# First Q and K weights issued by ScalarE, VectorE's constants first, and a new written order of all engines

## The chip, the cores and the metric

The kernel runs on one core of a Trainium2 chip. The metric is the device time of one execution in microseconds; the kernel before takes 200.04 (median of 3 runs, 199.62 to 200.08). One further execution was taken with the hardware profiler.

The core has TensorE (PE, matrix products; PEld is its weight load), VectorE (DVE), ScalarE (ACT), GpSimd (POOL), and SyncE (SP), which here issues the DMAs. Each engine works through its own instructions in order.

## The reference

Two branches work on the same input x (A_x) and are mixed by a gate:

```python
qkv = (x @ wqkv)                              # x: 2048 x 512, 32 heads of 16
scores = einsum("bhqd,bhkd->bhqk", q, k) * 16 ** -0.5
scores = where((0 <= i - j) & (i - j < 256), scores, -1e9)
a = (softmax(scores) @ v) @ wo                # sliding window of 256
h = layernorm(x)
u = gelu(einsum("bsd,sf->bdf", h, w1) + b1)   # 2048 -> 1376, over tokens
b = transpose(einsum("bdf,fs->bds", u, w2) + b2)
g = sigmoid((x * gate_w).sum(-1))
out = g * a + (1 - g) * b
```

## The kernel before

**Tiling.** The 2048 tokens are 16 tiles of 128. Projections work on four blocks i of 512 tokens: `q{k}_{i}` and `k{k}_{i}` for four groups k of eight heads, and `v{t}` for each tile t. Each is a chain of four matmuls over 128 rows of the weights, accumulated in one PSUM bank (`chain`, L691). In block 0 the first matmul is split into two halves of 256 columns, so that its steps `.0` and `.1` need different halves of x. Copies bring the results out: `kc`, `vc` and `xtc` (`copy_out`, L637, on VectorE or ScalarE) and `qc` (VectorE, L792).

**Attention.** For each tile j, scores `s{j}.v0` to `.v3` and the corner `s{j}.C` go to pairs of PSUM banks; ScalarE takes the exponential of each pair (`e...`, L932); VectorE or GpSimd puts zeros outside the window (`m...`, L945, L1012, L571); the products with V (`pv{j}.n`, L1125) follow. V parts that must lie on other partitions are moved by DMA within SBUF: `vs{t}` (L756) and `vz{j}` (L766), which wait for the V tiles that they move. VectorE then normalises and transposes the result (`n1` to `n4`, `nz`, L1216 to L1251) for the product with `wo`.

**The other branch.** `bs`, `ba`, `pow`, `h` are the layernorm. `u0` to `u10` multiply h by w1 over the tokens; `ub` adds the bias; one `gelu` task (L1291) works on all of them in place. It needs another table of ScalarE than the exponentials. `y{t}` multiplies by w2, and its last four matmuls by wo, so one bank holds both branches; `f{t}` scales and `o{t}` stores. The gate is the VectorE product `gl{t}` (L860) with a copy of gate_w on all partitions (`gw`, loaded at L542), a sum in the same instruction, then a small exponential `gatee`.

**The order.** Every piece of work is a `Task` with its engine's cost. The order on each engine, the choice of VectorE, ScalarE or GpSimd where there is one, and the bank or buffer (the digits behind the colon) are written out in `PLAN` (L217). [...] The costs are no instructions. On an engine the order is exactly that of `PLAN`: a task whose input is late holds everything behind it, and this goes for SyncE's queue of loads too.

**The start.** SyncE issues x in two halves of a block (x0.0, x0.2: tokens 0 to 255 and 256 to 511), then wqk0 to wqk3, each 128 rows of the Q and K weights (256 KB), with x1.4 (512 KB) between wqk2 and wqk3; then gw, wv and the DMA transposes xt1, xt3, xt2 of the other blocks. TensorE warms up on zeros (`warm`, five matmuls of 512 columns), transposes block 0 itself (`xta0.n.g`: half n of x, half g of its columns), with three matmuls on zeros (`warmb`) between the halves, and goes into the projections of block 0.

Of the kernel before, what the change touches and what calls it, by code (L numbers as in the profile page):

```python
# [9 lines left out]
ACT = mybir.ActivationFunctionType  # L10
# [92 lines left out]

def arrange(tasks):
# [21 lines left out]
    while len(order) < len(tasks):  # L126
# [92 lines left out]
        warm:5 xta0.0.1:4 xta0.0.0:3 warmb xta0.1.1:4 xta0.1.0:5 q2_0.0:6 q3_0.0:0 k1_0.0:2 k3_0.0:3  # L219
        k0_0.0:1 q1_0.0:5 q1_0.1 k2_0.0:7 q0_0.0:4 k2_0.1 q2_0.1 k0_0.1 q0_0.1 k3_0.1 k0_0.2 q0_0.2 k1_0.1  # L220
        q0_0.3 k3_0.2 q1_0.2 k3_0.3 q1_0.3 q3_0.1 q2_0.2 k1_0.2 q1_0.4 k1_0.3 q0_0.4 k0_0.3 k3_0.4 q2_0.3
        k0_0.4 q3_0.2 q2_0.4 k2_0.2 k1_0.4 k2_0.3 k2_0.4 v1.0:1 q3_0.3 q3_0.4 s0.v0:24 v1.2 v0.0:7 q3_1.0:6
        v0.2 q3_1.2 s0.C:24 v5.0:0 k2_1.0:7 k2_1.2 v5.2 s-1.C:24 v3.0:6 v14.0:7 v14.2 s1.v3:04 biast:3 v3.2
        q1_1.0:7 q1_1.2 s1.v0:02 v2.0:6 v2.2 v12.0:4 v12.2 v4.0:5 v4.2 pv-1.0:0 s0.v1:26 k3_1.0:4 k3_1.2
        k3_2.0:5 s1.v2:06 k3_2.2 v6.0:2 q0_1.0:3 q0_1.2 v6.2 pv0.0:0 pv0.1 pv0.2 s1.v1:46 v7.0:3 v7.2
        v15.0:2 s2.v1:06 v15.2 k0_2.0:5 v13.0:4 k0_2.2 v13.2 k1_1.0:3 s1.C:06 k2_2.0:2 k2_2.2 k1_1.2
        s2.v3:06 k0_1.0:5 k0_1.2 v10.0:2 v10.2 pv1.0:0 pv1.1 pv1.2 pv1.3 s2.v0:46 pv1.4 v8.0:2 v8.2 v9.0:3
        v9.2 s2.v2:06 q2_1.0:5 k1_2.0:4 q2_1.2 s2.C:20 k1_2.2 u0.0:6 u0.2 v11.0:7 v11.2 s3.v1:40 u0.4 u0.6
        u0.8 s3.C:02 u2.0:7 u0.10 u2.2 u0.12 u2.4 s3.v2:42 pv2.0:0 u0.14 pv2.1 pv2.2 pv2.3 u2.6 u2.8
        s3.v0:24 u1.0:6 u1.2 u1.4 s3.v3:02 u1.6 u1.8 u2.10 s4.v0:42 u2.12 u1.10 u2.14 u1.12 u1.14 s4.v1:04  # L230
        pv3.0:2 pv3.1 pv3.2 pv3.3 u3.0:7 u3.2 u3.4 s5.v2:04 u3.6 u3.8 u3.10 s4.v3:20 u3.12 u3.14 u4.0:6 u4.2
        s4.v2:24 q0_2.0:7 q0_2.2 u4.4 s4.C:40 u4.6 u4.8 u4.10 s6.v0:02 u4.12 q3_2.0:7 u4.14 pv4.0:4 pv4.1
        pv4.2 pv4.3 s5.v0:02 u5.0:6 q3_2.2 u5.2 u5.4 s5.v1:42 u5.6 u5.8 q2_2.0:7 q2_2.2 s5.C:02 u5.10 u5.12
        u5.14 s6.C:04 u6.0:7 u6.2 u6.4 s6.v2:02 u6.6 u6.8 q1_2.0:6 q1_2.2 u6.10 s5.v3:04 u6.12 u6.14 u7.0:6
        s6.v1:02 u7.2 u7.4 pv5.0:4 pv5.1 pv5.2 pv5.3 s6.v3:02 u7.6 u7.8 k3_3.0:7 k3_3.2 s7.v0:04 u7.10
        pv6.0:2 pv6.1 u7.12 pv6.2 pv6.3 s7.v1:04 u8.0:7 u7.14 u8.2 s7.v3:02 u8.4 k1_3.0:6 k1_3.2 s7.C:04
        u8.6 u8.8 q0_3.0:6 s7.v2:42 q0_3.2 u8.10 u8.12 u8.14 s8.v3:20 u9.0:6 u9.2 u9.4 s8.C:04 u10.0:7 u10.2
        u10.4 s8.v1:24 u9.6 u9.8 u10.6 u9.10 s8.v0:20 u9.12 u10.8 u9.14 s8.v2:42 u10.10 pv7.0:0 pv7.1
        q1_3.0:6 u10.12 u10.14 q1_3.2 s10.v0:24 pv7.2 k2_3.0:7 k2_3.2 pv8.0:2 pv8.1 k0_3.0:6 pv8.2 pv8.3
        pv7.3 k0_3.2 q2_3.0:4 q2_3.2 q3_3.0:5 y4.0:6 y0.0:7 q3_3.2 s9.v1:02 y0.2 y0.4 y4.2 y4.4 y0.6 y4.6  # L240
        y0.8 y0.10 s9.v3:40 y0.11 y0.13 y4.8 s9.v2:02 y4.10 y4.11 y2.0:7 y2.2 s9.C:40 y2.4 y4.13 y2.6
        s9.v0:24 y2.8 y2.10 y7.0:6 y2.11 s10.C:04 y2.13 y7.2 y7.4 s10.v3:02 y7.6 y8.0:7 y8.2 s11.v3:04 y8.4
        y7.8 pv9.0:2 pv9.1 pv9.2 pv9.3 s10.v2:04 y7.10 y8.6 y8.8 y8.10 s10.v1:02 y8.11 y8.13 y7.11 s11.C:04
        y7.13 y1.0:7 y1.2 y1.4 s11.v2:02 y5.0:6 y1.6 y5.2 s11.v1:24 y1.8 y5.4 y5.6 s13.v3:20 y1.10 y5.8
        pv10.0:4 pv10.1 pv10.2 y1.11 y1.13 y5.10 pv10.3 s12.v2:02 y5.11 y9.0:7 y5.13 s12.v0:04 y9.2 y9.4
        y9.6 s11.v0:02 y10.0:6 y10.2 y10.4 y9.8 s12.v1:24 y9.10 y10.6 y10.8 y9.11 s12.v3:04 y10.10 pv11.0:2
        pv11.1 pv11.2 pv11.3 y9.13 y10.11 y10.13 s13.v0:04 y6.0:7 y6.2 y3.0:6 s12.C:24 y3.2 y3.4 y3.6
        s13.C:04 y3.8 y6.4 y3.10 y6.6 s13.v1:24 y3.11 pv12.0:0 pv12.1 pv12.2 y3.13 pv12.3 s14.v3:24 y6.8
        y11.0:6 y11.2 y6.10 s13.v2:04 y6.11 y6.13 y11.4 s14.v2:42 y11.6 y11.8 y11.10 y11.11 s14.v0:40
        y13.0:7 y11.13 pv13.0:2 pv13.1 pv13.2 pv13.3 s14.v1:04 y12.0:6 y12.2 y12.4 s14.C:24 y12.6 y13.2  # L250
        y12.8 s15.A:04 y13.4 y13.6 y12.10 y12.11 y13.8 s15.C:02 y12.13 pv14.0:4 pv14.1 pv14.2 s15.B:20
        y13.10 y13.11 pv14.3 y14.0:6 y14.2 y14.4 y15l.0:1 y13.13 y14.6 y14.8 pv15.0:4 pv15.1 pv15.2 y14.10
        y15r.0:3 y15l.2 y15l.4 y14.11 y15r.2 y14.13 y15r.4 y15l.6 y15l.8 y15r.6 y15l.10 y15l.11 y15l.13
        y15r.8 y15r.10 y15r.11 y15m.0:2 y15r.13 y15m.2 y15m.4 y15m.6 y15m.8 y15m.10 y15m.11 y15m.13
    """,
    ACT="""
        xtc0.0.1 xtc0.0.0 kc3_0 kc0_0 kc1_0 kc2_0 e0.v0.0:5 e0.v0.1:4 vc0 vc1 e0.C.0:3 e0.C.1:2 kc2_1 vc5
        e-1.C.1:9 e-1.C.0:8 vc14 e1.v3.0:1 e1.v3.1:b e1.v0.0:a e1.v0.1:0 vc12 gatee0 vc4 e0.v1.1:8 e0.v1.0:9
        e1.v2.0:6 e1.v2.1:7 kc3_1 vc6 e1.v1.1:2 e1.v1.0:3 e2.v1.1:4 e2.v1.0:5 vc15 kc0_2 e1.C.0:d e1.C.1:c
        kc2_2 e2.v3.0:8 vc13 e2.v3.1:9 vc10 kc1_1 e2.v0.1:0 e2.v0.0:b vc8 e2.v2.0:1 e2.v2.1:7 e2.C.1:a kc1_2  # L260
        e2.C.0:d e3.v1.1:c e3.v1.0:6 e3.C.1:e e3.C.0:f e3.v2.1:0 e3.v2.0:b ub0 e3.v0.0:7 e3.v0.1:1 e3.v3.1:a
        e3.v3.0:5 e4.v0.0:4 e4.v0.1:d ub2 e4.v1.0:1 e4.v1.1:0 ub1 gatee2 e5.v2.0:c e5.v2.1:5 e4.v3.0:6
        e4.v3.1:f e4.v2.1:e e4.v2.0:7 e4.C.1:8 e4.C.0:9 e6.v0.1:2 e6.v0.0:3 e5.v0.1:4 e5.v0.0:d e5.v1.1:0
        gatee1 e5.v1.0:1 e5.C.0:7 e5.C.1:6 e6.C.0:e ub5 e6.C.1:f e6.v2.0:a e6.v2.1:b e5.v3.0:8 e5.v3.1:g
        e6.v1.0:9 e6.v1.1:h ub6 e6.v3.0:6 e6.v3.1:7 e7.v0.0:8 e7.v0.1:g kc3_3 e7.v1.0:a e7.v1.1:6 e7.v3.0:f
        e7.v3.1:b e7.C.1:e e7.C.0:7 e7.v2.1:9 e7.v2.0:h e8.v3.1:4 e8.v3.0:5 e8.C.1:c e8.C.0:d e8.v1.0:2
# [1146 lines left out]
```

## Time and profile before

| What | Value |
|---|---|
| median of 3 runs | 200.04 us |
| the profiled execution | 199.2 us |
| its span, first to last instruction | 197.5 us |
| TensorE matmuls busy | 187.4 us (95%), 4008 recorded |
| ScalarE busy | 169.9 us (86%) |
| VectorE busy | 157.8 us (80%) |
| GpSimd busy | 64.6 us (33%) |
| DMA | 22.01 MB, 111 GB/s on average |

The span is a little shorter than the execution, which has 1.7 us around it. Busy time of an engine is the union of its instructions' spans; successive matmuls overlap in the record, so the distance from start to start tells what one costs. In a row of the timeline, the columns are the start, the length, the engine, the line, the operation with what it writes and reads, the count, and in brackets the idle time before it and what ended that. In a row of a table by stretches, each engine has its busy time in that stretch and the number of its instructions; then come the granted TensorE clock (1.00 is full), the DMA share and the rate.

Some starts in the profiled execution, by the names above: warm 1.04, first transposes 3.67, first projection 5.82, first scores (s0.v0) 13.63, first u matmul 45.35, gelu 116.18, end of the last matmul 194.6.

### The profile page before, as it was taken

Reading aid. Unit: us, or ns where it says so; the run is one execution under the profiler, and the core shown is the slowest. Engines: PE = TensorE matmul, PEld = TensorE weight load, DVE = VectorE, ACT = ScalarE, POOL = GpSimd, SP = SyncE. Lnnn points to the kernel's source line nnn. Section 1 sums busy time; section 2 is a strip of 40 time slices with the busy share of each in tenths; the row PEclk is TensorE's granted clock in tenths of the full one; section 3 lists DMA queues with packets and bytes.
Section 4 is the critical chain, followed back from the end, with each engine's and each line's share of the span. In section 5 each row is a group of like instructions: output and inputs, shape, how many; then the busy total and the mean of one; then the engine's idle time right before and its main releaser. Section 6 shows DMA issues by size and latency. Waiting matters only on the chain.

```text
span 197.5 us, 9026 instructions
## 1 busy us (share of the span) xinstructions
PE 187.4 (95%) x4008; PEld 92.3 (47%) x4040; DVE 157.8 (80%) x340; ACT 169.9 (86%) x200; POOL 64.6 (33%) x102
## 2 busy tenths in 40 slices
PE   7999999999999999999999999899999999999994
PEld 3544344444535344456444563335345354454663
DVE  2699998799999897984767899177955775779893
ACT  3059998999899997999999899998998989899910
POOL 8922796563001122235200420222362320004520
PEclk9999999999999999999999999999999999999999
DMA  5986999942052811001496017001031002003022
GB/s 147 306 212 125 236 328 346 317 123 63 7 156 69 275 62 37 0 3 36 134 391 256 3 39 211 0 5 56 3 109 36 27 9 68 3 3 89 3 98 65
DMA packets 23444, 22.01 MB, mean 111 GB/s; under 512 B 7950, under 2 KB 21518, under 8 KB 23406
## 3 DMA queue, kind: packets, MB, share of 16 engines
q1 hardware_dynamic: 23406, 21.44, 36.1%
q8 instruction: 31, 0.51, 1.1%
q14 instruction: 7, 0.06, 0.1%
HBM read 15.61 MB, written 2.10 MB: 90 GB/s over the span
## 4 chain that ended last, share of the span: by engine, by line
PE 79%; ACT 11%; DVE 4%; issue 3%; DMA 2%; SPq 0%; ACTq 0%
PE pb L708 57%; PE ps L1125 10%; PE ps L980 9%; ACT et L932 7%; PE ps L1080 2%; ACT VA L640 2%; DMA wqkv<-in_A_wqkv_dram 2%; DVE stats L808 1%; ACT L932 1%; DVE et L1216 1%; DVE zt L1233 0%; SPq L489 0%; ACT ug L1291 0%; DVE h L824 0%; PE ps L1036 0%
## 5 line engine op out<-in xcount | busy, mean ns | idle before, releaser
L932 ACT ACTIVATE et<-ps 128x1024 bf16<-128x1024 f32 (+1 forms) x104 | 98.8, 1011 | 8.2 <-PE ps L980 5.5
L571 POOL TENSOR_SCALAR_AFFINE_SELECT et<-et 128x512 bf16<-128x512 bf16 (+3 forms) x60 | 41.6, 704 | 98.4 <-ACT et L932 65.7
L932 ACT ACTIVATE XT<-ps 128x1024 bf16<-128x1024 f32 (+1 forms) x50 | 49.1, 1028 | 1.2 <-PE ps L980 0.7
L708 PEld LDWEIGHTS <-wb 128*32 128x32 bf16 (+4 forms) x663 | 32.5, 97 | 37.0 <-issue 7.0
L708 PE MATMUL pb<-ug,wb 128*32 128x512 bf16 (+6 forms) x344 | 43.9, 365 | 0.9 <-issue 0.6
L708 PE MATMUL pb<-h,wb 128*32 128x512 bf16 (+2 forms) x301 | 41.9, 380 | 1.7 <-issue 1.7
L708 PE MATMUL pb<-XT,wqkv 128*128 128x512 bf16 (+2 forms) x166 | 31.8, 369 | 1.2 <-issue 0.8
L980 PE MATMUL ps<-QZ,KT 32*128 32x256 bf16 (+1 forms) x496 | 23.1, 265 | 0.9 <-ACT et L932 0.8
L1125 PEld LDWEIGHTS <-VA 128*32 128x32 bf16 (+1 forms) x1056 | 20.3, 97 | 6.2 <-issue 1.6
L792 DVE TENSOR_TENSOR QZ<-pb,par 128x1024 bf16<-128x1024 f32 x16 | 19.1, 1213 | 3.3 <-PE pb L708 2.4
L1125 PE MATMUL ps<-et,VA 128*32 128x128 bf16 (+2 forms) x760 | 21.7, 217 | 0.0
L1216 DVE STREAM_TRANSPOSE et<-ps 128x1024 f32<-128x1024 f32 (+1 forms) x13 | 15.7, 1207 | 4.2 <-PE ps L1125 3.7
L1012 DVE TENSOR_TENSOR et<-et,mask 128x512 bf16<-128x512 bf16 x38 | 16.9, 454 | 2.7 <-ACT et L932 2.7
L708 PEld LDWEIGHTS <-wqkv 128*128 128x128 bf16 (+1 forms) x172 | 12.0, 97 | 13.7 <-DMA wqkv<-in_A_wqkv_dram 0.9
L571 POOL TENSOR_SCALAR_AFFINE_SELECT XT<-XT 128x512 bf16<-128x512 bf16 (+1 forms) x15 | 9.8, 659 | 24.5 <-ACT XT L932 13.5
L708 PE MATMUL pb<-wo,xo 128*32 128x512 bf16 (+3 forms) x152 | 17.5, 369 | 0.4 <-issue 0.3
L980 PEld LDWEIGHTS <-KT 32*128 32x128 bf16 x496 | 7.4, 92 | 21.7 <-ACT et L932 12.1
L708 PE MATMUL pb<-wqkv,XT 128*128 128x512 bf16 x60 | 15.8, 380 | 0.6 <-issue 0.3
L1012 DVE TENSOR_TENSOR XT<-XT,mask 128x512 bf16<-128x512 bf16 x20 | 9.7, 485 | 6.4 <-ACT XT L932 6.4
L808 DVE BATCH_NORM_STATS2 stats<-xo 128x6 f32<-128x512 bf16 x16 | 10.6, 675 | 4.2 <-DMA xo<-in_A_x_dram 4.2
L1125 PEld LDWEIGHTS <-VZ 128*32 128x32 bf16 x832 | 13.2, 97 | 0.4
L1125 PE MATMUL ps<-XT,VA 128*32 128x128 bf16 (+2 forms) x296 | 12.7, 217 | 0.1
(77 smaller groups left out, 201.7 us busy)
## 6 DMA issues: line engine op xcount, KB each, us to landing
wb<-in_B_w_dram SPq DMA_DIRECT2D x18, 512.0 KB, 6.6
VZ<-VA SPq DMA_DIRECT2D x26, 70.0 KB, 2.5
xo<-in_A_x_dram SPq DMA_DIRECT2D x3, 512.0 KB, 5.0
wb<-in_B_w_dram SPq DMA_DIRECT2D x4, 352.0 KB, 7.5
out_dram<-ot SPq DMA_DIRECT2D x11, 128.0 KB, 1.8
wqkv<-in_A_wqkv_dram SPq DMA_DIRECT2D x4, 256.0 KB, 5.4
xo<-in_A_x_dram SPq DMA_DIRECT2D x2, 256.0 KB, 2.9
wqkv<-in_A_wqkv_dram SPq DMA_DIRECT2D x1, 512.0 KB, 7.7
```

What stands on the lines that cost most here:

```text
L571: return nc.gpsimd.affine_select(out=out_, in_=in_, pattern=[[0, n] for n in pattern] + [[step, HB]], compare_op=op, fill=0.0, base=base_, ...
L640: return nc.scalar.activation(out_(), in_(), ACT.Copy)
L708: made.append(nc.tensor.matmul(buf(b)[c:z_, c0:c0 + w_], lhsT=lhsT[:, c:z_], rhs=rhs, start=(j == 0), stop=(j == n - 1), skip_group_check= ...
L792: lambda k=k, b=b: nc.vector.tensor_tensor(out=QZ[:, k, :, (i % NQ) * SB:(i % NQ + 1) * SB], in0=buf(b)[:, None, :].to_broadcast([P, 2, SB ...
L808: f"bs{t_}", {"DVE": 0.67}, lambda b=b, t_=t_: nc.vector.bn_stats(buf(b)[:], xo[:, t_, :]),
L932: lambda e=e, b=b, shape=shape: nc.scalar.activation(out=shape(buf(e)), in_=shape(buf(b)), func=ACT.Exp, scale=SCALE),
L980: made.append(nc.tensor.matmul(to[:, :, done:done + m], lhsT=keys(j if x == "A" else j - 1, k)[rows], rhs=q[rows], start=True, stop=True, ...
L1012: made.append(nc.vector.tensor_tensor(out=v, in0=v, in1=m.to_broadcast(list(v.shape)), op=ALU.mult))
L1080: made.append(nc.tensor.matmul(buf(b2[r // 2])[m_:m_ + HB, at:at + P], lhsT=keys(t_, k)[rows, a:a + HB], rhs=q[rows], start=True, stop=Tru ...
L1125: return lambda: nc.tensor.matmul(to(), lhsT=v() if callable(v) else v, rhs=buf(e)[rows, col:col + n], start=first, stop=last, tile_positi ...
L1216: lambda: nc.vector.transpose(out=view(buf(tr).bitcast(FP32)), in_=view(buf(o))), [last], takes=[tr], uses=[o],
```

## The change

1. `const` and `zeros` come first on VectorE, `const` (three memsets) ahead of `zeros`. Their tasks are defined earlier in the code.
2. wqk0 is issued by ScalarE, as its first instruction, and waits for `const`. wqk1 to wqk3 stay on SyncE and follow x0.2 directly; x1.4 comes behind gw, xt1 and wv.
3. `warm` has six matmuls in place of five; `warmb` is gone.
4. Planner costs differ: score matmuls, gelu (6.6 in place of 7.0), the loads of x and of the weights, the latency of w2 loads.
5. All lists of `PLAN` and the set `THEN` are new. 21 copies, biases and outputs change between ScalarE and VectorE, 24 masks go from GpSimd to VectorE and 38 from VectorE to GpSimd. The V moves vz and vs stand in other places among the loads on SyncE.

The lists of `PLAN` are shown by their parts that the text speaks of.

```diff
 def cost_of(t, e):
     if e == "PE":
-        return c - 0.02 if t.mode == "s" else c * 0.738 if t.mode == "c" else c
+        return c - 0.01 if t.mode == "s" else c * 0.738 if t.mode == "c" else c
...
     PE="""
-        warm:5 xta0.0.1:4 xta0.0.0:3 warmb xta0.1.1:4 xta0.1.0:5 q2_0.0:6 q3_0.0:0 k1_0.0:2 k3_0.0:3
-        k0_0.0:1 q1_0.0:5 q1_0.1 k2_0.0:7 q0_0.0:4 k2_0.1 q2_0.1 k0_0.1 q0_0.1 k3_0.1 k0_0.2 q0_0.2 k1_0.1
...
-        k0_0.4 q3_0.2 q2_0.4 k2_0.2 k1_0.4 k2_0.3 k2_0.4 v1.0:1 q3_0.3 q3_0.4 s0.v0:24 v1.2 v0.0:7 q3_1.0:6
+        warm:5 xta0.0.0:3 xta0.0.1:4 xta0.1.0:5 k1_0.0:0 k0_0.0:1 xta0.1.1:7 q0_0.0:3 k2_0.0:2 q1_0.0:4
+        q1_0.1 q0_0.1 k2_0.1 k1_0.1 q1_0.2 k1_0.2 q1_0.3 k1_0.3 k3_0.0:5 q2_0.0:7 q0_0.2 q1_0.4 k2_0.2
+        k2_0.3 k0_0.1 q0_0.3 k0_0.2 k0_0.3 k0_0.4 k2_0.4 q2_0.1 q2_0.2 q3_0.0:6 k1_0.4 q0_0.4 k3_0.1 q2_0.3
+        q3_0.1 q3_0.2 k3_0.2 q3_0.3 q2_0.4 k3_0.3 k3_0.4 s0.v0:02 q3_0.4 q3_1.0:4 k2_1.0:5 k2_1.2 v0.0:3
...
-        u10.4 s8.v1:24 u9.6 u9.8 u10.6 u9.10 s8.v0:20 u9.12 u10.8 u9.14 s8.v2:42 u10.10 pv7.0:0 pv7.1
-        q1_3.0:6 u10.12 u10.14 q1_3.2 s10.v0:24 pv7.2 k2_3.0:7 k2_3.2 pv8.0:2 pv8.1 k0_3.0:6 pv8.2 pv8.3
-        pv7.3 k0_3.2 q2_3.0:4 q2_3.2 q3_3.0:5 y4.0:6 y0.0:7 q3_3.2 s9.v1:02 y0.2 y0.4 y4.2 y4.4 y0.6 y4.6
-        y0.8 y0.10 s9.v3:40 y0.11 y0.13 y4.8 s9.v2:02 y4.10 y4.11 y2.0:7 y2.2 s9.C:40 y2.4 y4.13 y2.6
+        s8.v1:26 u9.6 u10.6 u10.8 s8.v0:06 u9.8 u10.10 u9.10 s8.v2:26 u9.12 pv7.0:0 pv7.1 pv7.2 u10.12 u9.14
+        u10.14 s10.v0:62 pv7.3 q2_3.0:4 k0_3.0:5 pv8.0:2 q2_3.2 q3_3.0:0 k0_3.2 q3_3.2 pv8.1 pv8.2 pv8.3
+        q1_3.0:1 y4.0:6 y0.0:7 q1_3.2 k2_3.0:0 y0.2 k2_3.2 s9.v1:42 y0.4 y0.6 y0.8 y0.10 y0.11 y4.2 y4.4
+        s9.v3:04 y4.6 y0.13 y4.8 s9.v2:42 y4.10 y2.0:7 y2.2 y2.4 s9.C:20 y4.11 y4.13 y2.6 s9.v0:24 y2.8
...
-        y12.8 s15.A:04 y13.4 y13.6 y12.10 y12.11 y13.8 s15.C:02 y12.13 pv14.0:4 pv14.1 pv14.2 s15.B:20
-        y13.10 y13.11 pv14.3 y14.0:6 y14.2 y14.4 y15l.0:1 y13.13 y14.6 y14.8 pv15.0:4 pv15.1 pv15.2 y14.10
+        y12.8 y12.10 y12.11 y12.13 s15.C:26 pv14.0:0 pv14.1 pv14.2 pv14.3 s15.B:26 y13.10 y13.11 y14.0:5
+        y14.2 y13.13 y14.4 y14.6 y14.8 pv15.0:0 pv15.1 pv15.2 y15l.0:6 y14.10 y14.11 y15l.2 y15r.0:4 y14.13
...
     ACT="""
-        xtc0.0.1 xtc0.0.0 kc3_0 kc0_0 kc1_0 kc2_0 e0.v0.0:5 e0.v0.1:4 vc0 vc1 e0.C.0:3 e0.C.1:2 kc2_1 vc5
+        wqk0 xtc0.0.1 xtc0.1.0 kc0_0 kc2_0 kc1_0 kc3_0 e0.v0.1:0 e0.v0.0:4 kc2_1 e0.C.1:1 e0.C.0:5 vc0 vc5
...
     DVE="""
-        zeros bs0:0 ba0 bs3:1 const bs1:0 parity ba3 xtc0.1.0 xtc0.1.1 ba1 bs2:1 ba2 bs5:0 bs6:1 ba5 bs7:0
-        qc0_0 qc1_0 qc2_0 qc3_0 h1 gl3 qc3_1 h2 gl0 h3 ba7 gl1 gl2 biasc vc3 ba6 gatem0 qc1_1 bs4:0 vc2 ba4
+        const zeros bs1:0 xtc0.0.0 ba1 parity bs3:0 xtc0.1.1 bs0:1 ba3 ba0 bs2:0 qc1_0 gl2 gl3 qc0_0 ba2
+        qc2_0 qc3_0 gl1 h1 bs7:0 gl0 bs5:1 gatem0 h3 ba7 qc3_1 ba5 biasc bs6:0 m-1.C.0 h2 h0 qc1_1 ba6 vc12
...
-        x0.0 x0.2 wqk0 wqk1 wqk2 x1.4 wqk3 gw wv xt1 bias xt3 vs0 x2.8 vs1 xt2 w1_21 x3.12 w1_00 w1_01 w1_10
-        w1_02 w1_20 vs2 w1_23 w1_12 w1_11 vz4:1 w1_03 vz8:0 vz2:2 vz3:2 w1_13 w1_22 vz5:2 wo w2_0 w2_3 vz6:1
-        vz11:2 vz7:1 w2_1 w2_4 w2_2 w2_7 w2_6 w2_5 w2_8 vz10:0 w2_9 w2_10 vz9:1 o2 o4 o7 o0 o8 vz13:1 vz12:0
+        x0.0 x0.2 wqk1 wqk2 wqk3 gw xt1 wv x1.4 xt3 bias x2.8 vs0 xt2 w1_23 x3.12 vs1 vz2:1 w1_01 w1_21 vs2
+        w1_03 w1_10 w1_00 vz6:0 w1_02 wo vz5:2 w1_11 w1_20 vz3:1 w1_22 w1_12 w1_13 w2_1 vz4:1 vs13 vz8:1
+        w2_3 w2_2 w2_7 vz7:0 vz10:2 w2_5 w2_0 w2_4 w2_8 w2_9 w2_10 w2_6 o0 vz11:0 vz9:1 vz12:1 o8 o7 o2 o5
...
-    dqk = [
-        load(f"wqk{c}", lambda c=c: nc.sync.dma_start(wqkv[:, c, 0:2 * D], A_wqkv[c * P:(c + 1) * P, 0:2 * D]),
-             0.85 if c else 1.65, 2.6)
-        for c in range(4)
-    ]
+    def load_qk(c, start):
+        return lambda: start(wqkv[:, c, 0:2 * D], A_wqkv[c * P:(c + 1) * P, 0:2 * D])
+
+    dqk = [add("wqk0", {"ACT": 0.5}, load_qk(0, nc.scalar.dma_start), [k0], lat=3.0)]
+    dqk += [load(f"wqk{c}", load_qk(c, nc.sync.dma_start), 1.2 if c == 1 else 0.85, 2.6) for c in range(1, 4)]
...
-    add("warm", {"PE": 2.2}, lambda: warming(5, 512), [kz], takes=[wu], ins=10)
+    add("warm", {"PE": 2.62}, lambda: warming(6, 512), [kz], takes=[wu], ins=12)
...
-            between = add("warmb", {"PE": 0.64}, lambda: warming(3, 256), [t], uses=[wu], ins=6)
...
-    gelu = add("gelu", {"ACT": 7.0}, emit_gelu, ub)
+    gelu = add("gelu", {"ACT": 6.6}, emit_gelu, ub)
```

## The prediction

> **What bounds the kernel now.** I read the table by stretches first, since the page's one share per engine (PE 95%) hides where the other 5% is.
>
> ```profile
> core 0: us, PE busy (x) PEld busy (x) DVE busy (x) ACT busy (x) POOL busy (x), PEclk, DMA share, GB/s
> 0.00:14.00 14.00, 12.22 (x74) 6.05 (x76) 8.87 (x23) 4.54 (x7) 9.78 (x21) 1.00 0.82 234
> 14.00:45.00 31.00, 29.73 (x447) 13.08 (x451) 28.97 (x73) 29.88 (x43) 18.53 (x29) 1.00 0.84 237
> 45.00:112.00 67.00, 64.96 (x1474) 31.69 (x1487) 56.19 (x123) 62.44 (x73) 14.16 (x22) 1.00 0.33 109
> 112.00:126.00 14.00, 13.21 (x285) 6.40 (x285) 11.75 (x25) 13.81 (x14) 3.21 (x5) 1.00 0.32 88
> 126.00:186.00 60.00, 58.77 (x1489) 28.98 (x1501) 44.72 (x86) 56.51 (x63) 16.24 (x21) 1.00 0.11 34
> 186.00:197.50 11.50, 8.54 (x255) 6.13 (x244) 7.31 (x14) 2.71 (x4) 2.65 (x4) 1.00 0.22 71
> ```
>
> TensorE is the bound in every stretch; it idles 10.1 us in all, of which about 1 is before its first matmul and 2.9 after its last (194.6 of 197.5). Nothing else can be won: the change keeps the arithmetic, so a perfect order would save little more than 2 us after the start. Next the start, TensorE's rows in time.
>
> ```profile
> 1.04 2.31 PE L626 MATMUL pb<-ug 128*128 128x512 bf16 x5 [1.04 <-DVE ug L553]
> 3.67 1.03 PE L646 MATMUL pb<-ident,xo 128*128 128x128 bf16 x8 [0.31 <-DMA xo<-in_A_x_dram]
> 4.50 0.59 PE L626 MATMUL pb<-ug 128*128 128x256 bf16 x3
> 5.82 3.98 PE L708 MATMUL pb<-XT,wqkv 128*128 128x256 bf16 x25 [0.23 <-DMA wqkv<-in_A_wqkv_dram]
> 9.99 2.75 PE L708 MATMUL pb<-XT,wqkv 128*128 128x512 bf16 x12 [0.19 <-issue]
> ```
>
> The first projection waits for the first Q/K weights (issued by SyncE at 1.82, landed 3.95 later by the chain of waits), and there is a second hitch at 9.80, where the fourth weight quarter lands (issued 3.75, median 6.0 for these loads). The eight projections are then limited by TensorE itself. VectorE and the small gate load complete the picture of the start:
>
> ```profile
> 11.13 4.60 DVE L792 TENSOR_TENSOR QZ<-pb,par 128x1024 bf16<-128x1024 f32 x4
> gwr<-in_gate_w_dram SPq DMA_DIRECT2D x1, 128.0 KB, 6.9
> ```
>
> Last the gelu, the one place where TensorE visibly waits for ScalarE:
>
> ```profile
> 116.18 4.66 ACT L1291 ACTIVATE ug<-ug 128x1536 bf16<-128x1536 bf16 x3
> 121.37 1.28 ACT L932 ACT_TABLE_LOAD   x1
> 123.75 0.40 PE L980 MATMUL ps<-QZ,KT 32*128 32x256 bf16 x8 [0.38 <-ACT et L932]
> 125.58 0.40 PE L980 MATMUL ps<-QZ,KT 32*128 32x256 bf16 x8 [0.25 <-ACT et L932]
> ```
>
> **The change part by part: the start.** VectorE now writes its constants first (three memsets, 0.14 end to end in the rows at 5.09), so warming starts at 1.18, not 1.04. Six warm matmuls at the 0.42 between their starts reach 3.73: the transposes begin 0.06 later than now. The three fill matmuls (0.47 between 4.50 and 4.97) go, so the second group of transposes can start near 4.6; its half of x has landed by then (VectorE reads it at 4.48 without waiting). First projection: about 5.0.
>
> The weights must be there. ScalarE issues wqk0 when the constants are done, about 1.1. By the row (3.95 from issue to landing) that is 5.05. [...] The table load (1.28) that ScalarE does now at 0.79 comes after its DMA issue and is done near 2.9; its first copy is at 4.8, so it is covered.
>
> What decides is the fourth quarter. On SyncE the 512 KB of x1.4 leave the place in front of it (x1.4 now goes behind gw, xt1 and wv). At the 298 GB/s of the stretch from 5 to 10 us that is 1.7 us: 9.75 becomes about 8.1; I take 8.3. In the new order q1_0.4 is the first to need it. Behind it, up to the first scores s0.v0, stand 17 steps of 512 columns (0.2155) and 5 of 256 (0.108), with q1_0.4 itself 4.4 us: s0.v0 at 12.7. VectorE agrees: q1 complete at 8.7, its Q copy 1.21 (L792 row: 4.60 for four), then two gate products (0.68 each, L860), then the Q copy of q0, 1.21: 12.6. Now s0.v0 starts at 13.63 with one V half more done (0.43) and q3_0.4 done, which the new order still owes (0.22). So 12.92 against 13.20: **-0.3**. Bounds: -0.6 if the quarter lands before 7.7; the loss side is the second rival. wv then follows the transpose xt1, whose issue held SyncE 7.1 us now until the backlog before it was gone (12.55, wv landed at 12.6). The backlog shrinks by x1.4 and wv, 1 MB or 3.4 us, so xt1 should let go near 9 and wv land near 12.5; v0 wants it at about 14. x2.8 and the others behind move earlier too, and no wait of theirs appears.
>
> **V moves on SyncE.** vz2 now stands before eleven of the twelve w1 loads and waits for vc3 (ScalarE, about 22); vz6 waits for vc7 (36 to 40) and holds w1_02 behind it. w1_02 then lands by about 45; u0.8, the first to need it, comes near 49.8 (u0.0 is at 45.35 now). Covered by about 5 us. vz3 holds w1_22, w1_12 and w1_13 until pv2 is done (53), landing by 60; u4.8 needs them at 64. In return w2_8 to w2_10 have no V move between them (vz10 held the last two until 117), so they land near 115, not 122. I count nothing for these but the 0.1 by which y0.10 waits for w2_10 at 122.97, and put that into the next part.
>
> **The gelu.** The two waits cost TensorE 0.38 and 0.25, and about 0.07 each since successive groups otherwise overlap: 0.77. In the new order the last scores ahead of the gelu (s10.v0) come before q1_3 (0.86) and behind pv7.2 (0.22): 0.64 earlier, with the start 0.9. ScalarE idles 0.5 at this place now (before 110.30), so its exponentials can follow; the gelu starts near 115.2, the first exponentials behind it end near 115.2 + 5.17 + 1.31 + 1.02 = 122.7. s9.v1 has one more y step before it (0.43), and six and a half steps and the 0.33 of its own scores follow until s9.v3: about 123. It doesn't wait. s9.v2, 1.3 later, needs the third exponential (124.5) and just makes it. With w2_10 up to 0.87; I take **-0.6**, keeping a little for what just makes it. Bounds: -0.9, and +0.5 if the gelu doesn't move (six and a half steps cover less than the eight of now).
>
> **The tail.** From pv14.3 VectorE runs a chain of normalisations without a hole (186.77 to 192.69) that y14 and y15 wait for; TensorE loses some 0.4 between 190.8 and 192.2. The new order puts s15.B, y13.10 and y13.11 (1.2) behind pv14.3, which covers the chain; one corner mask (m15.C.0, 0.68 by the mean of its kind) comes into the chain. 1.2 less 0.7 is more than 0.4: **-0.4**. f14 and the left part of f15 go to ScalarE, idle there.
>
> **More turns.** TensorE's groups in different tilings cost a turn. The rows price it:
>
> ```profile
> 56.47 0.40 PE L980 MATMUL ps<-QZ,KT 32*128 32x256 bf16 x8
> 56.80 1.47 PE L708 MATMUL pb<-h,wb 128*128 128x512 bf16 x6
> 63.89 0.40 PE L980 MATMUL ps<-QZ,KT 32*128 32x256 bf16 x8
> 64.45 1.24 PE L708 MATMUL pb<-h,wb 128*128 128x512 bf16 x5 [0.16 <-issue]
> ```
>
> Scores between two untiled chains take 0.33 to the next start; scores that follow tiled work (61.12 to 63.89) and precede an untiled chain take 0.56. Entering scores costs 0.095 from untiled and 0.105 from tiled work. Counting both written orders: tiled-scores-untiled 13 against 11 (+0.45), untiled to tiled 5 against 3 (+0.19), scores entered from tiled work 20 against 17 (+0.32) and from untiled 38 against 41 (-0.29). Together **+0.7**. This is certain work, and speaks against the change.
>
> **The rest.** Net 14 masks go from VectorE (0.48) to GpSimd (0.68), which is busy 33%; each lies several exponentials (0.92) ahead of its pv. The edits of planner costs make no instruction; they count only as order. New small waits in the reordered middle, where 14 to 45 now holds some 1.5 us of 0.2 us waits, I can't cost: -0.5 to +1.5, taken as 0.
>
> Sum: -0.3 - 0.6 - 0.4 + 0.7 = -0.6 on the profiled execution's 199.2 (span 197.5 and 1.7 around it), 198.6. The median of the runs is 200.04, 0.84 above that execution; so 199.4.
>
> **Rivals.** *No change.* The gelu waits return in another place, because ScalarE is 99% busy there (13.81 of 14.00) and an order doesn't make it faster: -0.3 - 0.4 + 0.7, with 0 for the gelu, is 200.0. For it: TensorE's 13.21 there can't shrink. Against it: the 0.5 hole of ScalarE before 110.30.
>
> *Slower: the gate load in front of q0.* VectorE now does two gate products between the Q copies of q1 and q0. They need gw, which took 6.9 us from issue (4.30) and landed at 11.2. With x1.4 gone I have it at 9.5; needed at 9.95. From there each us late delays qc0_0, then s0.v0, with TensorE's in-order queue behind it. If it lands at 11.2 as now, +1.25: 200.6; if it shares the engines with the transpose now issued right behind it and lands at 12, +2: 201.4. For it: the late landing now, in 128 rows behind 2 MB. It decides from a landing of about 11.2 on.
>
> **How the numbers follow.** 0.3% of 200 is 0.6 us, about what a measurement can tell from no change. Forecast 0.45 (its time at the upper end of the gain side, since the uncosted waits lean up), no change 0.27, slower 0.28 (gate load, or the uncosted +1.5 on top of no change: 200.7 to 201.8). The bounds -0.6, -0.9, -0.4 on one side give 198.2 with the turns; on the other 201.6. So 198.1 to 201.6; the forecast's own range is 198.1 to 199.9.
>
> **What would show it.** First projection near 5.0, first scores at or before 12.8 (now 13.63), with VectorE not waiting for gwr; gelu near 115.2; no ScalarE wait above 0.2 before the scores behind it; TensorE busy near 188; GpSimd near 74. I am wrong if gwr lands after 10, if scores after the gelu still wait, or if new waits of TensorE between 14 and 110 sum to over 1 us more.

## The result, and the profile after

The changed kernel takes 198.57 us (median of 20 runs, 197.77 to 200.36), the kernel before beside it 199.58 (20 runs, 198.93 to 203.25): ratio 0.9939 with a 95% interval of 0.9920 to 0.9958. Measured again in the second group of experiments it took 198.31 against 199.50, ratio 0.9922 (0.9905 to 0.9940). So it is 1.0 to 1.2 us faster. The forecast was 0.64 below the median then known, 199.4, inside a range of 198.1 to 201.6; the direction and the range held. The measured time lies 0.8 below the forecast; of that, 0.46 is the base, since the median of three runs (200.04) stood above that of 20 (199.58). The sum behind the forecast did not hold: each of its four terms was off, and that they add up to -0.6, close to the -0.5 between the two first profiles, is luck.

The table by stretches, of the changed kernel's first profile (span 197.0; the columns are those of the table shown for the kernel before):

```profile
core 0: us, PE busy (x) PEld busy (x) DVE busy (x) ACT busy (x) POOL busy (x), PEclk, DMA share, GB/s
0.00:14.00 14.00, 12.38 (x71) 6.71 (x72) 8.72 (x23) 4.47 (x8) 9.18 (x21) 1.00 0.92 236
14.00:45.00 31.00, 31.00 (x454) 13.04 (x453) 28.98 (x71) 29.93 (x45) 19.55 (x32) 1.00 0.80 222
...
112.00:126.00 14.00, 14.00 (x281) 6.71 (x274) 11.76 (x22) 13.63 (x13) 0.68 (x2) 1.00 0.23 68
```

TensorE seems to have no idle time left between 14 and 126 us, where the kernel before had 1.3 in the second stretch and 0.8 in the fourth. Only part of that is real, as the experiments show: the matmul records of this profile are complete and those of the kernel before were not.

The start and the scores behind the gelu, in the timeline of TensorE in the same profile:

```profile
1.18 2.74 PE L626 MATMUL pb<-ug 128*128 128x512 bf16 x6 [1.18 <-DVE ug L488]
4.36 1.46 PE L646 MATMUL pb<-ident,xo 128*128 128x128 bf16 x12 [0.44 <-DMA xo<-in_A_x_dram]
5.61 0.63 PE L705 MATMUL pb<-XT,wqkv 128*128 128x256 bf16 x2
...
13.38 0.40 PE L977 MATMUL ps<-QZ,KT 32*128 32x256 bf16 x8
...
123.25 0.40 PE L977 MATMUL ps<-QZ,KT 32*128 32x256 bf16 x8
124.98 0.40 PE L977 MATMUL ps<-QZ,KT 32*128 32x256 bf16 x8
```

No row of the start waits for weights any more, but the transposes wait for x (0.44), and the first projection comes at 5.61, not at 5.0. wqk0 was issued by ScalarE at 0.80, before the first memset of `const` began (0.87), and landed at 3.77: the program has no wait for `const` here (that wait, which the text ahead of the prediction tells, is only in the planner). With wqk0 under way beside it x came later: x0.0 landed at 4.31 against 3.63 before, x0.2 at 5.03 against 4.33. The fourth quarter landed at 8.10 (forecast 8.3, before 9.72), the gate weights at 8.57 (forecast 9.5, before 11.2), so the rival of the late gate load did not come up. The two scores behind the gelu have no wait in brackets, where they had 0.38 and 0.25.

The gelu itself, in ScalarE's timeline of this profile:

```profile
109.81 1.94 ACT L929 ACTIVATE et<-ps 128x1024 bf16<-128x1024 f32 x2 [0.57 <-PE ps L1122]
112.31 1.02 ACT L929 ACTIVATE XT<-ps 128x1024 bf16<-128x1024 f32 x1 [0.56 <-PE ps L977]
...
115.56 4.66 ACT L1288 ACTIVATE ug<-ug 128x1536 bf16<-128x1536 bf16 x3
```

It starts at 115.56 (forecast 115.2, before 116.18). ScalarE still has its hole of half a microsecond in front of the exponentials of s8.v2 (109.81), and a second one of 0.56 in front of those of s10.v0.

**Where the time went.** At some groups of scores exactly the same steps stand ahead in both written orders, apart from the warming, so their starts can be compared directly. Four of them, the starts in us (the third row is from the changed kernel's second profile, run e5 below):

| | s1.v0 | s3.v1 | s8.v1 | s9.v2 | end of the last matmul |
|---|---|---|---|---|---|
| before | 21.70 | 47.17 | 105.14 | 125.58 | 194.59 |
| after, first profile | 22.09 | 46.91 | 104.85 | 124.98 | 194.05 |
| after, second profile | 21.12 | 45.97 | 103.92 | 124.04 | 193.11 |

The rows of s8.v1, before and after:

```profile
105.14 0.40 PE L980 MATMUL ps<-QZ,KT 32*128 32x256 bf16 x8
104.85 0.40 PE L977 MATMUL ps<-QZ,KT 32*128 32x256 bf16 x8
```

From s1.v0 to s3.v1 the changed kernel takes 24.82 and 24.85 in its two profiles, in place of 25.47: 0.6 won. From s3.v1 to s8.v1 nothing changes (57.94 and 57.95 against 57.97). From s8.v1 to s9.v2, the gelu's stretch, it takes 20.13 and 20.12 in place of 20.44: 0.3 won. Behind that 0.06 is lost. Only the start differs between the two profiles: 0.4 lost in one, 0.6 won in the other. That is what the first experiments are about.

The profile of the kernel before is a lucky one at its start. Three runs below (e4, e7, e10) change nothing so early and have s1.v0 at 22.55, 22.64 and 23.39 in place of 21.70. Of the lead, 0.3 is lost again by s3.v1: the six other profiles of the old order take 25.12 to 25.15 for that way. So a gain of 0.3 in the middle belongs to the new order and the other 0.3 to this one profile.

### The profile page after: what moved, and what is told of

It reads as the page before. It is cut to its first block, busy times and chain, and to the rows that moved or that the text cites. A ratio compares the mean times of both kernels' runs of the same rounds, so it can differ in the third digit from the quotient of the medians.

```text
span 197.0 us, 9082 instructions
## 1 busy us (share of the span) xinstructions
PE 192.4 (98%) x4049; PEld 92.9 (47%) x4049; DVE 156.3 (79%) x327; ACT 169.4 (86%) x199; POOL 78.3 (40%) x117
## 4 chain that ended last, share of the span: by engine, by line
PE 96%; DMA 2%; DVE 0%; issue 0%
PE pb L705 71%; PE ps L1122 11%; PE ps L977 10%; PE ps L1077 3%; DMA xo<-in_A_x_dram 2%; PE pb L646 1%; PE ps L1033 0%; DVE ot L476 0%; PE pb L591 0%
## 5 line engine op out<-in xcount | busy, mean ns | idle before, releaser
L929 ACT ACTIVATE et<-ps 128x1024 bf16<-128x1024 f32 (+1 forms) x107 | 101.7, 1014 | 8.6 <-PE ps L977 6.2
L571 POOL TENSOR_SCALAR_AFFINE_SELECT et<-et 128x512 bf16<-128x512 bf16 (+3 forms) x67 | 50.3, 762 | 64.5 <-ACT et L929 31.6
L929 ACT ACTIVATE XT<-ps 128x1024 bf16<-128x1024 f32 (+1 forms) x47 | 45.4, 1016 | 1.9 <-PE ps L977 1.1
L705 PE MATMUL pb<-ug,wb 128*32 128x512 bf16 (+5 forms) x354 | 45.3, 367 | 0.0
L705 PE MATMUL pb<-h,wb 128*32 128x512 bf16 (+2 forms) x320 | 44.5, 381 | 0.0
L705 PE MATMUL pb<-XT,wqkv 128*128 128x512 bf16 (+2 forms) x172 | 32.6, 374 | 0.0
L571 POOL TENSOR_SCALAR_AFFINE_SELECT XT<-XT 128x512 bf16<-128x512 bf16 (+1 forms) x23 | 15.2, 664 | 36.7 <-ACT XT L929 12.9
L476 DVE TENSOR_SCALAR ot<-pb,c,c 128x512 bf16<-128x512 f32 (+1 forms) x11 | 8.1, 738 | 11.2 <-PE pb L705 10.9
L1009 DVE TENSOR_TENSOR et<-et,mask 128x512 bf16<-128x512 bf16 x32 | 15.1, 477 | 2.3 <-ACT et L929 2.3
L1122 PE MATMUL ps<-et,VZ 128*32 128x64 bf16 x512 | 13.7, 193 | 0.0
```

Source lines behind the costliest of these rows:

```text
L476: return nc.vector.tensor_scalar(out=out_, in0=in_, scalar1=scale, scalar2=bias, op0=ALU.mult, op1=ALU.add)
L571: return nc.gpsimd.affine_select(out=out_, in_=in_, pattern=[[0, n] for n in pattern] + [[step, HB]], compare_op=op, fill=0.0, base=base_, ...
L705: made.append(nc.tensor.matmul(buf(b)[c:z_, c0:c0 + w_], lhsT=lhsT[:, c:z_], rhs=rhs, start=(j == 0), stop=(j == n - 1), skip_group_check= ...
L929: lambda e=e, b=b, shape=shape: nc.scalar.activation(out=shape(buf(e)), in_=shape(buf(b)), func=ACT.Exp, scale=SCALE),
L1009: made.append(nc.vector.tensor_tensor(out=v, in0=v, in1=m.to_broadcast(list(v.shape)), op=ALU.mult))
L1122: return lambda: nc.tensor.matmul(to(), lhsT=v() if callable(v) else v, rhs=buf(e)[rows, col:col + n], start=first, stop=last, tile_positi ...
```

## The experiments

### The start: who issues wqk0, where x1.4 stands

> The changed kernel with one part undone: wqk0 is issued by SyncE again, right behind x0.2; all orders are otherwise those of the change. Theory A (wqk0 on ScalarE's queue is first on the shared DMA engines and pushes x back): x0.0 lands near 3.65 again instead of 4.31, wqk0 near 5.8 instead of 3.77, TensorE's place at 10 us is 0.3 to 0.7 earlier than in the changed kernel, and the time is 0.3 to 0.7 lower, 197.9 to 198.3. Theory B (the earlier first weights are what makes the change faster): the first projection waits for wqk0 until 5.8 and the time rises by 0.3 to 0.5, to about 199.0.

```diff
     ACT="""
-        wqk0 xtc0.0.1 xtc0.1.0 ...
+        xtc0.0.1 xtc0.1.0 ...
     SP="""
-        x0.0 x0.2 wqk1 wqk2 wqk3 gw xt1 ...
+        x0.0 x0.2 wqk0 wqk1 wqk2 wqk3 gw xt1 ...
```

Measured: 199.32 us (12 runs, 198.12 to 200.84), ratio to before 0.9976 (0.9946 to 1.0006). The profile was of the fastest of these runs, 198.12, and looked as good as the changed kernel's: wqk0 at 5.67, x0.0 at 3.51, s1.v0 at 21.56. The median said otherwise. One profile could not decide this, so it was put beside the changed kernel again (e6 below).

> The changed kernel with x1.4 back between wqk2 and wqk3 on SyncE, nothing else. If taking x1.4 out of the way of the fourth weight quarter is worth what the prediction said (1.7 us of data), wqk3 lands at 9.5 to 9.8 instead of 8.1, q1_0.4 waits about 0.8 (now at 8.85), and the time rises by 0.5 to 0.9. If the rest of TensorE's queue absorbs it, by under 0.2.

```diff
-        x0.0 x0.2 wqk1 wqk2 wqk3 gw xt1 wv x1.4 xt3 ...
+        x0.0 x0.2 wqk1 wqk2 x1.4 wqk3 gw xt1 wv xt3 ...
```

Measured: 199.67 us, ratio 0.9994 (0.9972 to 1.0017), so most of the gain is gone with this one load. TensorE's waits in that run:

```profile
PE pb L705 <- DMA wqkv<-in_A_wqkv_dram: 1.2, 1, 1.2
```

The fourth quarter landed at 9.45, and one wait of 1.2 for it is back. s0.v0 starts at 14.03, in place of 13.38 and 12.40 in the two profiles of the changed kernel, though the clock came early in this run (4.96 us). x1.4's place is worth about 1 us in the new order, more than the prediction gave the whole start.

> The kernel before with one part of the change alone: wqk0 issued by ScalarE, nothing waits for it there; warming, fill matmuls and all orders as before. Theory A: x0.0 lands at 4.3 instead of 3.63 and x0.2 at 5.0, the transposes begin 0.7 later, first projection near 6.2; the time rises by 0.3 to 0.8. Theory B: first projection at 5.0 to 5.4, the time falls by 0.3 to 0.5.

```diff
     ACT="""
-        xtc0.0.1 xtc0.0.0 kc3_0 ...
+        wqk0 xtc0.0.1 xtc0.0.0 kc3_0 ...
     SP="""
-        x0.0 x0.2 wqk0 wqk1 wqk2 x1.4 wqk3 ...
+        x0.0 x0.2 wqk1 wqk2 x1.4 wqk3 ...
```

Measured: 200.48 us, ratio 1.0041 (1.0025 to 1.0058). In the old program the same edit makes it 0.8 us slower. wqk0 came at 3.72, x0.0 at 4.25, and with five warm matmuls TensorE stood idle for 0.93 in front of the transposes; the full clock was granted only at 8.0 us. One more loss came later: y0.10 waited for the last load of W2.

```profile
4.29 1.03 PE L646 MATMUL pb<-ident,xo 128*128 128x128 bf16 x8 [0.93 <-DMA xo<-in_A_x_dram]
124.67 0.39 PE L708 MATMUL pb<-ug,wb 96*128 96x512 bf16 x1 [0.85 <-DMA wb<-in_B_w_dram]
```

> The kernel before with the 512 KB of x1.4 moved from in front of the fourth weight quarter to behind wv and xt1. Theory A (x1.4's place is worth 1 us, as taking it back in the changed kernel showed): the fourth quarter lands near 8.2 to 9.3, its wait of 0.4 goes, 0.3 to 1.0 us faster than before. Rival (in the old order the first quarter, 5.7 to 7.1 from SyncE, limits the projections): within 0.3% of before.

```diff
-        x0.0 x0.2 wqk0 wqk1 wqk2 x1.4 wqk3 gw wv xt1 bias ...
+        x0.0 x0.2 wqk0 wqk1 wqk2 wqk3 gw wv xt1 x1.4 bias ...
```

Measured: 206.89 us, ratio 1.0338 (1.0295 to 1.0381). Neither expectation had a loss of 7 us in it. The waits of VectorE in the first 24 us of that run (what waited, for what: total, how often, longest):

```profile
DVE stats L808 <- DMA xo<-in_A_x_dram: 10.1, 2, 7.6
```

The waits of TensorE over the whole span:

```profile
PE ps L980 <- DVE QZ L792: 6.1, 1, 6.1
```

And the stretch behind it in the table by stretches:

```profile
16.00:24.00 8.00, 4.23 (x18) 1.42 (x18) 6.78 (x10) 2.21 (x3) 1.05 (x2) 0.57 0.16 37
```

The old order of VectorE has statistics of x1.4 (bs5, bs6, bs7) in front of the first Q copies (qc0_0 to qc3_0). With x1.4 late VectorE stood for it 7.6 us, the Q copies stood behind, and TensorE waited 6.1 us for QZ at the first scores. The granted clock was half from 16.5 to 23.3 us, so TensorE, at work again from 19.8, ran at half clock for 3.5 us (0.57 in the row is the mean granted clock of the stretch). It fell 2.9 us after the last matmul had ended (13.6), within the idle of 6.1; the longest idle of TensorE between two matmuls in the other profiles is 1.3 (e4). So the move of x1.4 in the changed kernel rests on another edit, which the prediction listed without seeing what it carries: the new VectorE order takes bs5 to bs7 behind the Q copies.

### The same start again, side by side

> The changed kernel once more, beside the others of this group. Theory A (the start is worth 0.3 only when TensorE's clock is granted early; in the profile after, it was granted at 7.11 instead of 4.69 and x landed 0.7 later, so that the first 14 us lost 0.7): a new profile has a new time of the grant, between 4.7 and 8; wqk0 lands near 3.75 and x0.0 near 4.3 again; ratio 0.994 again. Theory B (missing records are the whole of TensorE's 'issue' idle): where this profile has all of its matmul records, no issue idle is shown; where about 30 are missing, some 24 idles of 0.16 us are, at an equal span.

Nothing is edited. Measured: 198.31 us (197.72 to 198.43), ratio 0.9922 (0.9905 to 0.9940). Start rows of TensorE in this profile:

```profile
4.28 1.13 PE L646 MATMUL pb<-ident,xo 128*128 128x128 bf16 x12 [0.36 <-DMA xo<-in_A_x_dram]
5.32 0.38 PE L705 MATMUL pb<-XT,wqkv 128*128 128x256 bf16 x2
...
12.40 0.40 PE L977 MATMUL ps<-QZ,KT 32*128 32x256 bf16 x8
...
62.80 0.40 PE L977 MATMUL ps<-QZ,KT 32*128 32x256 bf16 x8
63.36 1.24 PE L705 MATMUL pb<-h,wb 128*128 128x512 bf16 x5 [0.16 <-issue]
```

The clock came at 4.40 us here and at 7.11 in the first profile. It can be read off the rows: the twelve transposes took 1.13 in place of 1.46, the first two projections 0.38 in place of 0.63. The first scores stand at 12.40 in place of 13.38. The same program thus has starts that differ by 1 us.

The last two rows settle the turns. The same place in the first profile:

```profile
63.74 0.40 PE L977 MATMUL ps<-QZ,KT 32*128 32x256 bf16 x8
64.07 1.47 PE L705 MATMUL pb<-h,wb 128*128 128x512 bf16 x6
```

Here it is x6, there x5 with "0.16 <-issue" in front and 0.23 later. Yet the next scores follow 1.73 behind these here (65.47) and 1.74 there (64.54): no time was lost, the record of one matmul is missing, and its time looks like an idle. The first profile of the changed kernel has all 4049 records and no such idle; the second has 4016, and in its list of TensorE's waits stands

```profile
PE pb L705 <- issue: 3.8, 24, 0.2
```

while that run was the faster one. The kernel before had 4008 of 4040 records and as many idles, 24 of 3.8 us in all; the 0.16 in the prediction's row at 64.45 (x5) is one of them.

> The changed kernel with the first Q and K weights issued by SyncE behind both halves of x, beside the changed kernel itself. Theory A (ScalarE's issue costs as much as it wins, since x then lands 0.7 later): within 0.3% of the changed kernel, on either side, with x0.0 at 3.5 and wqk0 at 5.7. Rival (ScalarE's issue is what brings the gain of the start): 0.5 us and more above the changed kernel, in every round.

The edit is that of e1. Measured: 199.47 us (12 runs, 198.53 to 200.90), ratio 1.0003 (0.9978 to 1.0027), 1.16 above the changed kernel in the same group; its fastest run lies above the slowest of e5. TensorE waited for the first weights:

```profile
6.06 0.39 PE L705 MATMUL pb<-XT,wqkv 128*128 128x256 bf16 x2 [0.86 <-DMA wqkv<-in_A_wqkv_dram]
```

So ScalarE's issue is worth about 1.2 us in the new order. Whether wqk0 as the first load in SyncE's own queue would do the same was not run: issuing engine and place in the queue changed together. wqk0 landed at 6.01 in this profile. Over all profiles of this case it landed between 5.67 and 7.07 when SyncE issued it as its third load (seven profiles), and between 3.67 and 3.80 when ScalarE issued it (seven profiles); x0.0 came some 0.7 later in the latter (4.23 to 4.36 against 3.42 to 3.69). From SyncE the wait can thus be up to 1 us longer than the 0.86 shown. That this makes the spread of 2.4 us over the 12 runs is argued, since the runs without a profile show no landing.

> The changed kernel with seven warm matmuls in place of six, so that TensorE has no idle time between 3.9 and the landing of x at 4.3. Theory A (the idle 0.44 in front of the transposes is what lets the clock be granted late): the grant comes at 5.3 or before, the first projections run at the full clock, 0.3 to 0.6 us faster than the changed kernel. Rival (the grant goes its own way, whatever TensorE does in that gap): the grant again anywhere between 4.7 and 8, and the same time as the changed kernel within 0.3.

```diff
-    add("warm", {"PE": 2.62}, lambda: warming(6, 512), ...
+    add("warm", {"PE": 3.05}, lambda: warming(7, 512), ...
```

Measured: 198.09 us (197.98 to 198.23), ratio 0.9920 (0.9906 to 0.9934). That is 0.2 below the changed kernel, less than the intervals can tell apart. The clock was granted at 4.64 us. The transposes start at 4.41, as late as x allows, without an idle. The six runs lie within 0.25 us, against 0.7 (6 runs) and 2.6 (20 runs) in the two sets with six warm matmuls.

> The kernel before with the first Q and K weights on ScalarE and seven warm matmuls in place of five (with five it was 0.4% slower than before). Theory A (the earlier weights pay only where TensorE has warm matmuls until the later x is there, so that the clock is granted early): grant before 5.5, start at least 0.5 earlier than in the run with five, 0.5 to 1.2 us faster than that run, so ratio 0.998 to 1.0. Rival (in the old order the weights' place doesn't pay whatever the warming, since the fourth quarter behind x1.4 limits): ratio 1.002 to 1.004 as with five.

The edit is e3's and seven warm matmuls in place of five. Measured: 199.53 us, ratio 0.9967 (0.9936 to 0.9997): 0.4 faster than the kernel before, where e3 was 0.8 slower, with the clock granted at 4.63. So in the old order early weights cost time with five warm matmuls and pay with seven, which last until the later x is there. Not all of this difference is at the start: y0.10 waited 0.85 for W2 in e3 and 0.48 here. The old order with seven warm matmuls and wqk0 still on SyncE was not run, so what the warming alone is worth stays open.

### The gelu: what moved it

> The kernel before with one move in TensorE's order: the last scores ahead of the gelu, s10.v0, go in front of q1_3, as in the change. The prediction's step: the gelu starts 0.6 to 0.9 earlier (116.18 before) and the waits of 0.38 and 0.25 of the scores behind it shrink to 0.2 or less together; the time falls by 0.4 to 0.6. Rival (ScalarE is the limit there, an order doesn't change it): the gelu starts within 0.2 of now, the waits stay, the time within 0.2.

```diff
-        q1_3.0:6 u10.12 u10.14 q1_3.2 s10.v0:24 pv7.2 ...
+        u10.12 u10.14 s10.v0:24 q1_3.0:6 q1_3.2 pv7.2 ...
```

Measured: 199.95 us, ratio 1.0026 (1.0002 to 1.0050). s10.v0 stood for its bank, which the exponentials of s8.v2 held until 112.74:

```profile
112.79 0.40 PE L980 MATMUL ps<-QZ,KT 32*128 32x256 bf16 x8 [0.64 <-ACT et L932]
```

The two waits behind the gelu are gone, but this one stands in their place, and nothing was won: s8.v1 to s9.v2 takes 20.81, against 20.44 before.

> The kernel before with pv7.0 and pv7.1 ahead of u10.10 and with s10.v0 ahead of q1_3: the order that the changed kernel has in front of the gelu, in the old program. Theory A (what moves the gelu is that pv7.1 frees the buffer of exponentials for e8.v2 and with it the bank for s10.v0): ScalarE's hole of 0.5 before e8.v2 shrinks to below 0.2, the gelu starts 0.4 to 0.6 earlier than 116.2 against the work before it, TensorE waits less than 0.2 in the scores behind it, 0.3 to 0.5 us faster than before. Rival (the order behind the gelu, one y step more ahead of s9, is what hides it): no change against before, the waits for ScalarE stay at 0.3 and more.

```diff
-        s8.v2:42 u10.10 pv7.0:0 pv7.1 q1_3.0:6 u10.12 u10.14 q1_3.2 s10.v0:24 pv7.2 ...
+        s8.v2:42 pv7.0:0 pv7.1 u10.10 u10.12 u10.14 s10.v0:24 q1_3.0:6 q1_3.2 pv7.2 ...
```

Measured: 200.56 us, ratio 1.0052 (1.0029 to 1.0075). pv7.0, put earlier, waited 0.31 for its bank, which the exponentials of s8.v0 held. The hole in ScalarE stayed at 0.46. s10.v0 waited 0.21 for ScalarE; behind the gelu the scores wait no longer, but y0.10 waited 0.47 for the last part of W2. From s8.v1 to s9.v2 it took 21.12, 0.7 more than before.

> The kernel before with kc3_3 and ub10 moved from ScalarE to VectorE and s10.v0 ahead of q1_3. Theory A (ScalarE's load on the way to the gelu sets it): the gelu 0.3 to 0.6 earlier against the work at 100 us, the two waits behind it (0.38 and 0.25) gone, 0.3 to 0.6 us faster than before. Rival (the chain from e8.v0 over pv7.1 to e8.v2 and the bank of s10.v0 sets it, not ScalarE's load): the gelu within 0.15 of where it was, the waits stay, no faster than before.

```diff
     PE: as in e4
     ACT="""
-        ... e7.v0.1:g kc3_3 e7.v1.0:a ... e8.v2.0:a ub10 e10.v0.0:6 ...
+        ... e7.v0.1:g e7.v1.0:a ... e8.v2.0:a e10.v0.0:6 ...
     DVE="""
-        m6.v1.1 m7.v0.1 ... n45 qc1_3 ...
+        m6.v1.1 kc3_3 m7.v0.1 ... n45 ub10 qc1_3 ...
```

Measured: 200.07 us, ratio 0.9994 (0.9966 to 1.0022). ScalarE's timeline there:

```profile
114.15 1.02 ACT L932 ACTIVATE et<-ps 128x1024 bf16<-128x1024 f32 x1 [0.56 <-PE ps L980]
115.45 1.02 ACT L932 ACTIVATE et<-ps 128x1024 bf16<-128x1024 f32 x1 [0.28 <-PE ps L1125]
```

Taking 1.28 us of copies off ScalarE brings nothing: it becomes a hole of 0.56 in which the scores of s10.v0 are awaited, and the second exponential waits another 0.28, for a product with V (L1125).

> The changed kernel with two copies in front of the gelu back on ScalarE, where the kernel before has them: kc3_3 (0.60) and ub10 (0.68). Theory A (the gelu comes earlier because ScalarE has less to do on the way to it): the gelu starts 0.3 to 0.6 later against TensorE's work at 100 us, waits for ScalarE of 0.2 to 0.4 come back in the scores behind it, 0.3 to 0.6 us slower than the changed kernel (ratio to before 0.994 to 0.996). Rival (the order of TensorE in front of the gelu sets it, the two copies fit into ScalarE's holes of 0.4 and 0.56): gelu less than 0.2 later, no waits, ratio as the changed kernel's, 0.992 to 0.994.

The same two copies put back on ScalarE in the changed kernel (kc3_3 behind gatee3, ub10 behind e8.v2.0). Measured: 198.69 us, ratio 0.9930 (0.9901 to 0.9958). The gelu starts 10.80 behind s8.v1, in place of 10.71 in the changed kernel, without a wait behind it. The copies fit into ScalarE's holes but for 0.09.

Counted from s8.v1, the gelu starts after 11.04 in the four profiles that have the old order there (before, e3, e11, e12), after 10.71 in all six that have the new one (after, e1, e2, e5, e6, e8), and after 11.25 to 11.30 in e4, e7 and e10. So neither ScalarE's load nor s10.v0's place alone brings the gelu forward; the whole new order does, by 0.33. The rows name a chain through both engines: the exponentials of s8.v0 free the bank of pv7.0; pv7.1 lets those of s8.v2 start; they free the bank of s10.v0; pv7.2 frees what its second exponential needs; then comes the gelu. Only the changed order has all of these in a row (s8.v2 with one step behind it, pv7.0, pv7.1, pv7.2, three steps, s10.v0). In e4, e7 and e10 pv7.2 still stood behind q1_3, and the 0.28 was the price. That the row of pv7.2 was the missing piece is read from these rows; the old order with pv7.2 moved as well was not run. Nor was the order in front of the gelu tried without the one behind it in the changed kernel.

The waits that went were 0.38 and 0.25, yet the stretch is only 0.3 shorter. The same steps thus take some 0.3 longer in the new order with no wait in their rows. That this is the price of more turns between tiled work (128*32 in the rows of its matmuls) and untiled work (128*128) is argued, not shown.

## Why the prediction was right, and where it was wrong

**The start, -0.3: wrong in its pieces.** The landing of wqk0 was sized with 3.95 from issue, the row of a load that stood third in SyncE's queue, plus a wait for `const` that does not exist: 5.05, where 3.77 was measured. wqk0, issued 1.03 earlier than from SyncE, landed 1.9 to 3.4 earlier, and the kernel was 1.2 us faster (e5 against e6), where the -0.3 was counted from the fourth quarter alone. With this load under way beside it x landed some 0.7 later, and the transposes were not given that delay. x1.4's move was the right step but undersized: 1 us, and it stands only because VectorE's statistics moved too (e12). What the start wins in a profile went with the grant of the clock: -0.6 (granted at 4.40) and +0.4 (at 7.11). And the profile that the -0.3 was counted from had an early start itself, 0.8 and more ahead of three others of the same start. The gains of e2 and e6 cannot be added: each removes a wait that hides part of the other's.

**V moves 0: right for w1, too small for w2.** w1_02 and the others were covered as worked out. The last two loads of W2 landed at 115.7 and 117.2 (forecast near 115, not 122). I gave that 0.1. In three profiles of the old order y0.10 waited for the last of them: 0.85 in e3, 0.48 in e11, 0.47 in e7; V moves held its issue until 119.05, 118.14 and 119.25. That the new place of vz10 keeps TensorE clear of this is argued from the landings; no run moves vz10 alone.

**The gelu, -0.6: the waits went as forecast, but 0.3 was won.** s9.v3 and s9.v2 "just make it". The reason given, that s10.v0 comes earlier and the exponentials follow, was incomplete: e4 did just that and was not faster. And 0.3 of the waits came back as dearer work in the same stretch.

**The tail, -0.4: wrong, 0.** From s14.v1 on, which again has the same work ahead of it in both orders, each takes 17.09 to the end of its last matmul. The "0.4 that TensorE loses between 190.8 and 192.2" were idles behind missing records; nothing was there to win. **More turns, +0.7: too large.** Its largest term (0.45) was the price of scores between tiled and untiled work, 0.56 against 0.33, and the 0.23 between them is one missing matmul. With complete records it is 0.33 for both. Of the rest (+0.2 by the count) nothing shows from s3.v1 to s8.v1 and 0.06 behind s9.v2; the 0.3 in the gelu's stretch may be it. For the same reason TensorE is busy 192.4 where I had 188. GpSimd's 78.3 against 74 is a size.

**The uncosted middle, taken as 0 in -0.5 to +1.5: -0.6 against the first profile of before, -0.3 against the others of its order.** The "1.5 us of 0.2 us waits" was mostly missing records too: e11 has the old order and all of its records, and TensorE waits there once for 0.2 between 14 and 45. What else makes the 0.3 was not traced.

The sum by its own steps for the first profile: start +0.39, middle -0.65, s3.v1 to s8.v1 -0.03, gelu -0.31, the stretch behind it +0.06, together -0.54 (198.67 against 199.2), where I had -0.6. Two artefacts of +0.7 and -0.4 stood in for a late clock and a middle that I couldn't cost. For the second profile: -0.58, -0.62, -0.02, -0.32, +0.06 is -1.48 (197.72 against 199.2), and the median change of 1.0 to 1.2 lies between. The lower end of the range was added up wrongly: -0.6 - 0.9 - 0.4 + 0.7 from 200.04 is 198.84, not 198.2. The measured 198.57 lies below that, and inside only with the -0.5 allowed for the middle.

## What to carry to other kernels

Compare the count of matmul records with the program before reading TensorE's small "issue" idles: the 0.16 in front of a group that is one short (x5 in e5, x6 in the first profile) was no idle, since the next scores followed after 1.74 and 1.73, and the price taken from such a row, 0.56, was 0.23 too high. A load that is moved back in a queue can hold up what stands behind the instruction that reads it (in e12 VectorE stood 7.6 us for x1.4, and TensorE waited 6.1 us behind it): ask of each engine what that is. And size the start from several profiles and the spread of the runs: the first scores started at 13.38 and 12.40 in two profiles of the same program, and one profile of the kernel before led three others of the same start by 0.8 and more. To compare two orders, look for instructions that have the same work ahead of them in both; a busy share does not tell tenths.

## What was not expected of the hardware

The full clock of TensorE was granted anywhere between 4.4 and 8.0 us over the profiles here, though TensorE began at 1.04 to 1.18 in all; the same program had it at 4.40 and 7.11. Counted from the first matmul, the grant came 3.2 (e5) to 7.0 us (e3) later; the longest idle of TensorE in between was 0.36 in the one and 0.93 in the other. With seven warm matmuls it was granted at 4.63 and 4.64 in both profiles taken; two are too few to call that a rule, since with six 4.40 was seen too.

The load of wqk0 issued by ScalarE at 0.80 was complete before that of x0.0, of the same 256 KB, which SyncE issued at 0.81 (3.77 against 4.31 in the first profile). In all seven profiles that have it the two issues lie within 0.01 us and wqk0 lands 0.5 to 0.6 first. Why stays open.
